# Gate and sum buffer in three parts, the copy out of PSUM ahead of the gate's mask, token loads in thirds, and second products dealt out by a plan

## The chip, the cores and the metric

One core of one Trainium2 chip runs the whole kernel. The metric is the device time of one execution in microseconds (us), as a median over runs. The engines are TensorE (PE, with its weight loads as PEld), VectorE (DVE), ScalarE (ACT), GpSimd (POOL) and SyncE (SP), which issues nearly all of the transfers.

## What is computed

```python
scores = scale * np.matmul(q, k.transpose(0, 1, 3, 2))        # 8 x 12 heads, 448 x 448, head_dim 64
scores = np.einsum('bhij,hg->bgij', scores, w_pre)            # heads are mixed before the softmax
attn = softmax(scores)                                         # max, exp, divided by the sum
attn = np.einsum('bhij,hg->bgij', attn, w_post)               # and mixed again after it
x = np.matmul(attn, v)  # -> 3584 tokens x 768
h = x @ w_in            # 768 -> 2048
g = h - np.tanh(h)      # the gate
out = g @ w_out         # 2048 -> 768
```

All is in float32. The kernel carries operands of matrix products as a high and a low part of a narrower type, and a product as three matmuls: high by high, high by low, low by high.

## The kernel before

The attention part fills the first 880 us or so of the span and is not touched; only its last places share the engines with the first block of the second part. The second part, the two large products with the gate between them, is where the change lies.

**Blocks.** The 3584 tokens are seven blocks of 512. Block 0 is computed plainly: 16 columns `f` of 128 hidden features, one after the other (`Block0.step`, L358). The six other blocks are taken in three pairs `s`, and a pair's two blocks and the halves of the weights go through a scheme with seven products in place of eight for a 2 x 2 split of the operands (Strassen-Winograd). Its operands, seven arrays called b11, b21, t2, t1, t3, b22, t4, are sums and differences of halves of the two blocks, each in a high and a low part.

**First products.** `pair_step` (L666) does one of eight steps `p` of a pair: seven products of nine matmuls each (three chunks of 128 rows, three matmuls a chunk) into two PSUM banks X and Y, in the order b11 X, b21 Y, t2 X, t1 Y, t3 X, b22 Y, t4 X. Some add to what is already in the bank, so a copy of X or Y on ACT or DVE has to have read the bank before the next product of that bank may start. The copy at L698 reads X after the third product (t2), and the fifth product (t3) waits for it. The weights of a product are one tile `wa` of 384 KB, loaded six products ahead (L626).

**Gate.** The gate of four hidden columns at a time is computed for two halves g1 and g2. The last parts of g1 and the whole of g2 run in the next step (`Late`, v0 to v5, L630 on): ACT does squares (L331, L332), the hyperbolic tangent (L336), another square (L337) and a mask (L347); DVE combines them (L340, L341, L344, L350) and overwrites the small arguments under the mask (L353). The tiles between them exist once each, so each engine waits for the other. In particular the mask (a3, L347) overwrites what L344 reads, so ACT gets to it only after DVE's L344. Four sums are then added (L655, L659, L660). Gate values and sums of one step are seven arrays of 128 x 512 in one tile `g` (1792 KB), of which there is one buffer. It is stored in DRAM (gs) by one transfer (L663, end of the step), and the next step's first write to it (L350 in v0) waits until that transfer has landed. In block 0 the first two arrays of the same tile take the gate of two columns, stored in go (L388).

**Second products.** The results are made of 200 units: 32 plain ones for block 0 and 56 for each pair. A unit is twelve matmuls into the banks y (L504 to L506, or L534 to L536). Two units share one weight tile `w` (768 KB, three buffers, L402, L418 or L421); two of a pair's units, or four plain ones, share one tile `gl` of gate values (512 KB, three buffers, L403 or L428), which ACT and DVE first split in a high and a low part (L448, L449). Loads are issued two tiles ahead. Results leave PSUM through tiles `c` and are stored by transfers of 192 KB (L519). The units of a pair can only run when the gate values of that pair are in DRAM, so the units of block 0 and of pair s fill PE during the steps of the pair after it.

**The order of the work** is written out by hand: each engine takes its instructions in the order in which the program calls them. After each product of a step, `rest(i)` runs `between(i)` (jobs that make the operands of the pair: `xq_jobs`, L570 on, eleven stages on ACT L576 and DVE L572, L579) and then a number of units. Before, a step of pair 0 gets 3 units, one of pair 1 or 2 gets 5.25 on the mean, and between two pairs stand 14 units (HELD 8 of the pair before, AHEAD 6 of the new one), into which the late gate's parts and five stages of the operands are dealt; the other stages run in step 0 of the next pair. In the tail, after the last pair, 14 such units and then 50 more run.

**Transfers.** SP issues in order. The token arrays of the next pair (five of 768 KB, L567) are loaded in the last step of a pair, each over two ranges of tokens (one where both lie in the same sequence), all three chunks in one transfer. The eight semaphores of SP's transfers are used in turn, so each issue first waits for the transfer eight before it. A load from gs waits for the stores of the same array region, and an issue that waits holds everything behind it.

Of the kernel before, what the change touches and what calls it, by code (L numbers as in the profile page):

```python
# [179 lines left out]
def kernel_body(  # L180
# [69 lines left out]

    ff = SimpleNamespace(w={}, x={}, xs={}, wa={}, w2={}, gr={}, gp={})

# [31 lines left out]
    def work(tag, n=2):  # L284
        return ff.rw.tile([P, n, TB], F32, name=tag, tag=tag)
# [70 lines left out]
    class Block0:  # L356
# [4 lines left out]
        def step(self, between=None):  # L361
# [19 lines left out]
            if f % 2:  # L381
                if old:
                    old.d2()
                    old.a3()
                    g = work("g", 7)[:, :2]
                    old.d3(g)
                    old.d4(g)
                    self.store = lambda: nc.sync.dma_start(gos[:, f - 3 : f - 1], g)  # L388
                self.old = Gate(self.h) if f < NF else None
            elif old:  # L390
                old.a1()
                old.a2()
                old.d1()


    class Results:
# [121 lines left out]
        def store(self, b, t, h, c):  # L518
            nc.sync.dma_start(  # L519
                out[b * TB + t * TT : b * TB + (t + 1) * TT, h * N2 : (h + 1) * N2], c.rearrange("p c n -> p (c n)")  # L520
            )

# [107 lines left out]
    class Late:  # L630
# [15 lines left out]

        def v3(self):
            self.g2.d2()
            self.g2.a3()
            self.g2.d3(self.g[:, 2:4])  # L650

        def v4(self):
            g = self.g
            self.g2.d4(g[:, 2:4])
            nc.vector.tensor_add(g[:, 4:6], g[:, 0:2], g[:, 2].unsqueeze(1).to_broadcast([P, 2, TB]))  # L655

        def v5(self):
            g = self.g
            nc.vector.tensor_add(g[:, 6], g[:, 1], g[:, 4])  # L659
            nc.vector.tensor_add(g[:, 2], g[:, 3], g[:, 6])  # L660

        def store(self):
            nc.sync.dma_start(gss[self.s][:, :, self.q], self.g)  # L663
            ff.stored[self.s] = self.q + 1

    def pair_step(s, q, late, units, between):  # L666
# [8 lines left out]
        def rest(i):  # L675
            between(i)
            res.units(units[i])

        X, Y = hbank(), hbank()
# [14 lines left out]
        if late:  # L694
            late.v2()
            late.v3()
        h23 = work("h23")
        nc.scalar.mul(h23[:, 0], X, -1.0)  # L698
        rest(2)

# [23 lines left out]
        g1.a3()  # L724
        if late:
            late.store()
        rest(6)
# [561 lines left out]

    def load_all_xq(s, names):  # L1290
        ba, bb = 2 * s + 1, 2 * s + 2
        for x, b, h in (("b11l", ba, 0), ("b21l", ba, 1), ("t3l", bb, 0), ("b22l", bb, 1), ("t4l", ba, 1)):
            if x in names:
                load_xq(x, b, h)

    xq = xq_jobs()
    res = Results()
    ff.n_wa, ff.stored = 0, [0] * NS

    def between0(f):  # L1300
        if 3 <= f <= 7:
            load_all_xq(0, (("b11l", "t3l", "b21l", "b22l", "t4l")[f - 3],))
# [12 lines left out]

    HELD, AHEAD = 8, 6
    late, left = None, 4 * NQ
    for s in range(NS):
        per_step = (left - HELD) / NQ
        due = 0.0  # L1320
        for p in range(NQ):

            def between(i):
                for _ in range(1 + (i == 0)):
                    next(xq, None)
                if p == NQ - 1 and s + 1 < NS:
                    for x, at in (("b11l", 0), ("b21l", 1), ("t3l", 4), ("b22l", 5), ("t4l", 6)):
                        if i == at:
                            load_all_xq(s + 1, (x,))

            units = []
            for i in range(7):
                due += per_step / 7
                units.append(int(due + 1e-6))
                due -= units[-1]
            late = pair_step(s, p, late, units, between)
        left = 7 * NQ - AHEAD
        if s + 1 < NS:
            xq = xq_jobs()
        jobs = [  # L1340
            [late.v0], [late.v1, late.v2], [late.v3], [late.v4], [late.v5, partial(next, xq, None)],
            [partial(next, xq, None)] * 2 + [late.store], [partial(next, xq, None)] * 2,
        ]
        for fs in jobs:
            for f in fs:
                f()
            res.units(2)
        late = None
    for _ in res.at:
        pass  # L1350

# [30 lines left out]
```

## Time and profile before

| | us |
|---|---|
| median of 3 runs (1884.4 to 1892.67) | 1887.47 |
| the profiled execution | 1885.07 |
| its span | 1883.3 |
| PE busy in it | 1724.8 |
| DVE busy | 1214.6 |
| ACT busy | 1146.1 |

The profiled execution lies 2.4 us below the median; its span is 1.8 us shorter than its time. Times in rows are us from the span's start; durations at the end of a group are in ns where it says "mean ns". A wait is told with the instruction that sat idle first and what released it behind the arrow. PEclk is the granted clock of TensorE as a share of full speed.

### The profile page before, as it was taken

The numbers are of one execution on the slowest core, as the hardware profiler recorded it, in microseconds if no ns is written. First come the engines' busy times: TensorE is split into PE (matmuls) and PEld (weight loads), VectorE is DVE, ScalarE is ACT, GpSimd is POOL, SyncE is SP. The second block draws the span as 40 slices with busy tenths as digits, with TensorE's granted clock in tenths as the row PEclk, the third lists the DMA queues.
The fourth block names the chain that finished last, engine by engine and source line by source line (L and its number), as shares of the span: only waits on it lengthen the run. The fifth ranks groups of instructions, "written<-read, shape, count | busy, mean of one in ns | idle before, by whom it ended". The sixth has DMA issues, their size and how long they took to land.

```text
span 1883.3 us, 40937 instructions
## 1 busy us (share of the span) xinstructions
PE 1724.8 (92%) x16068; PEld 1419.0 (75%) x16068; DVE 1214.6 (64%) x2119; ACT 1146.1 (61%) x2016; POOL 403.4 (21%) x574
## 2 busy tenths in 40 slices
PE   8999999999998999999968988888987988988898
PEld 6777777767776777777747777777877877877898
DVE  5776776676775776653867676757676767676333
ACT  5787777777786777674845554555554455555232
POOL 1454544544553454531000000000000000000000
PEclk9999999999998998999979999889999999999999
DMA  8769796887878597665956778858779858777897
GB/s 182 218 214 266 239 262 218 239 258 212 253 236 261 194 263 235 201 212 176 330 203 210 252 245 303 312 191 327 268 261 366 312 199 321 274 261 261 305 325 271
DMA packets 337743, 477.42 MB, mean 253 GB/s; under 512 B 103824, under 2 KB 262288, under 8 KB 337552
## 3 DMA queue, kind: packets, MB, share of 16 engines
q1 hardware_dynamic: 337244, 474.38, 77.0%
q8 instruction: 128, 2.10, 0.5%
q14 instruction: 63, 0.52, 0.1%
q10 hardware_dynamic: 308, 0.43, 0.1%
HBM read 277.09 MB, written 120.59 MB: 211 GB/s over the span
## 4 chain that ended last, share of the span: by engine, by line
PE 57%; DMA 17%; DVE 10%; ACT 9%; issue 3%; SPq 2%; POOL 2%; ACTq 0%; DVEq 0%; POOLq 0%
PE ps_o L951 12%; DMA gs<-g 8%; PE ps_m L993 7%; PE ps_p L912 7%; PE ps_q L868 5%; PE ps_h L315 4%; PE ps_h L316 4%; PE ps_h L318 4%; PE y L534 3%; PE y L536 3%; PE y L535 3%; DMA t<-s 2%; DMA w<-wo 2%; DMA vr<-in_v_dram 1%; DVE gl L449 1%
## 5 line engine op out<-in xcount | busy, mean ns | idle before, releaser
L951 PEld LDWEIGHTS ps_o<-wr,e 60*112 60x112 f32 (+1 forms) x5760 | 310.5, 177 | 43.1 <-POOL wr L934 18.4
L951 PE MATMUL ps_o<-wr,e 60*112 60x60 f32 (+1 forms) x5760 | 319.0, 261 | 15.7 <-ACT at L961 7.0
L921 DVE TENSOR_REDUCE mx<-ps_p 128x1 f32<-128x448 f32 x360 | 207.8, 619 | 184.0 <-PE ps_p L912 183.5
L923 ACT ACTIVATE e<-ps_p,mx 128x448 f32<-128x448 f32 x360 | 225.4, 633 | 97.4 <-DVE mx L921 95.4
L534 PE MATMUL y<-w,gh 128*128 128x384 f32 x672 | 231.4, 344 | 29.1 <-DMA w<-wo 14.0
L536 PE MATMUL y<-w,gl 128*128 128x384 f32 x672 | 230.1, 342 | 2.0 <-DVE gl L449 2.0
L535 PE MATMUL y<-w,gh 128*128 128x384 f32 x672 | 228.9, 341 | 0.0
L449 DVE TENSOR_TENSOR gl<-gl,gh 128x1024 fp32r<-128x1024 f32 x92 | 112.5, 1224 | 178.7 <-ACT gh L448 175.0
L961 ACT COPY at<-ps_o 112x960 f32<-112x960 f32 x156 | 153.8, 986 | 84.1 <-PE ps_o L951 83.5
L912 PE MATMUL ps_p<-t,wpre 60*64 60x448 f32 (+1 forms) x1440 | 184.1, 579 | 12.9 <-DMA t<-s 12.8
L993 PEld LDWEIGHTS ps_m<-at,vr 112*64 112x64 f32 x3072 | 150.4, 139 | 31.2 <-ACT at L968 12.4
L993 PE MATMUL ps_m<-at,vr 112*64 112x120 f32 (+1 forms) x3072 | 164.8, 264 | 8.3 <-ACT at L968 4.8
L448 ACT CAST gh<-gl 128x1024 fp32r<-128x1024 f32 x92 | 95.7, 1041 | 114.4 <-DMA gl<-gs 67.9
L331 ACT ACTIVATE u<-h 128x1024 f32<-128x1024 f32 x56 | 59.5, 1062 | 163.5 <-DVE h L708 83.1
L534 PEld LDWEIGHTS y<-w,gh 128*128 128x128 f32 x672 | 129.7, 193 | 37.7 <-ACT gh L448 23.9
L934 POOL TENSOR_TENSOR wr<-wpost,zs 128x120 f32<-128x120 f32 x180 | 70.3, 391 | 328.4 <-DVE zs L933 234.1
L535 PEld LDWEIGHTS y<-w,gh 128*128 128x128 f32 x672 | 129.8, 193 | 3.6
L536 PEld LDWEIGHTS y<-w,gl 128*128 128x128 f32 x672 | 128.9, 192 | 4.5 <-DVE gl L449 4.5
L347 ACT ACTIVATE qb<-u,bias 128x1024 f32<-128x1024 f32 x56 | 64.5, 1152 | 104.6 <-DVE qa L344 104.6
L868 PE MATMUL ps_q<-kk,qh 64*120 64x448 f32 (+1 forms) x768 | 126.3, 406 | 1.2 <-DVE kk L820 0.5
L868 PEld LDWEIGHTS ps_q<-kk,qh 64*120 64x120 f32 (+1 forms) x768 | 61.1, 179 | 86.0 <-issue 55.4
L873 DVE COPY s<-ps_q 120x448 f32<-120x448 f32 (+1 forms) x192 | 112.9, 616 | 14.2 <-PE ps_q L868 12.6
(174 smaller groups left out, 3376.2 us busy)
## 6 DMA issues: line engine op xcount, KB each, us to landing
t<-s SPq DMA_DIRECT2D x342, 210.0 KB
gs<-g SPq DMA_DIRECT2D x24, 1792.0 KB
gl<-gs SPq DMA_DIRECT2D x84, 512.0 KB
w<-wo SPq DMA_DIRECT2D x52, 768.0 KB
wa<-ss SPq DMA_DIRECT2D x96, 384.0 KB
w<-ts SPq DMA_DIRECT2D x48, 768.0 KB
wa<-wi SPq DMA_DIRECT2D x72, 384.0 KB
cr<-in_moe_w_in_dram SPq DMA_DIRECT2D x48, 256.0 KB
```

Of the source, the lines that this page charges most:

```text
L449: nc.vector.tensor_sub(lo, raw(lo), raw(hi))
L534: nc.tensor.matmul(y, gh[:, tok], wh, start=first, stop=False, skip_group_check=True)
L535: nc.tensor.matmul(y, gh[:, tok], wl, start=False, stop=False, skip_group_check=True)
L536: nc.tensor.matmul(y, gl[:, tok], wh, start=False, stop=last, skip_group_check=True)
L868: nc.tensor.matmul(ps[:n, :S], qx[a, hp, :], kx[a, hp % 2], start=(x == 0), stop=(x == 2))
L873: eng(sts[i][:n, 2 * hp + j, :], ps[:n, :S])
L912: nc.tensor.matmul(pss[r][halves[j], :], wpre[k, :], ts[j][k, :], start=True, stop=True)
L921: nc.vector.tensor_reduce(out=mx, in_=ps, axis=AX.X, op=ALU.max, negate=True)
L923: nc.scalar.activation(e, ps, AF.Exp, bias=mx, scale=1.0, accum_out=zs[:, 0, r : r + 1])
L951: nc.tensor.matmul(ps[:CP, j, c * GP : (c + 1) * GP].rearrange("p (h i) -> p h i", i=GI)[:, :, r * GH : (r + 1) * GH], e[k, c * CP : (c + ...
L961: nc.scalar.copy(ats[i0][:, :, :, at : at + 2 * GI].rearrange("p c h (j i) -> p j (c h) i", j=2), ps[:CP, :, : NC * GP].rearrange("p j (x ...
L993: nc.tensor.matmul(pv[j * D : (j + 1) * D, r, :n], vt[:, j, c, :], ats[i][:, c, 2 * hp + j, :n], start=(c == 0), stop=(c == NC - 1),)
```

## The change

1. The tile `g` of seven arrays becomes three: `ga` (two arrays, the gate g1), `gb` (two, the gate g2) and `gs` (three sums). Memory stays the same. `ga` is stored when two ticks have passed after v0, `gb` and `gs` two ticks after v5. In block 0 the gate alternates between `ga` and `gb`.
2. A tick passes after every unit and once at the end of each `rest`; `after(n, f)` puts off a call by n ticks. The stores of results (L519) are put off by two ticks too.
3. In `pair_step` the copy of X that was behind v2 and v3 (L698) is called between them, so on ACT it stands ahead of the mask.
4. Each token load is cut into its three chunks: `load_xq` issues six transfers where there were two, and they are dealt out two or so at a time.
5. Block 0 runs two more stages of the operands (columns 13 and 15). Between two pairs all eleven stages stand, two at a time.
6. The plan of the units: between pairs stand HELD + AHEAD = 18 and 18 units in place of 14, and 14 after the last pair. Step 0 of the three pairs gets 4, 6 and 5 units (FIRST); the other seven share 12, 34 and 37. So a step of pair 0 has one or two units where it had three, one of pair 1 four or five.

```diff
-                    g = work("g", 7)[:, :2]
+                    g = work(("ga", "gb")[f // 2 % 2])
...
+    def after(n, f):
+        ff.later.append([n, f])
+
+    def tick():
+        for x in ff.later:
+            x[0] -= 1
+        while ff.later and ff.later[0][0] <= 0:
+            ff.later.pop(0)[1]()
...
         def units(self, n):
             for _ in range(n):
                 next(self.at, None)
+                tick()
...
         def store(self, b, t, h, c):
...
+            after(2 if self.n_gr < len(self.grs) else 0, lambda: nc.sync.dma_start(to, c.rearrange("p c n -> p (c n)")))
...
         x_tiles(name)
-        for to, i, at in runs(b):
-            nc.sync.dma_start(raw(ff.xs[name])[:, :, to], xs[i][:, h * HK : (h + 1) * HK, at])
+        for c in range(HK):
+            for to, i, at in runs(b):
+                nc.sync.dma_start(raw(ff.xs[name])[:, c, to], xs[i][:, h * HK + c, at])
+            yield
...
         def v0(self):
-            self.g = work("g", 7)
+            self.ga = work("ga")
             self.g2.a1()
-            self.g1.d3(self.g[:, 0:2])
-            self.g1.d4(self.g[:, 0:2])
+            self.g1.d3(self.ga)
+            self.g1.d4(self.ga)
+            after(2, lambda: nc.sync.dma_start(gss[self.s][:, 0:2, self.q], self.ga))
...
         def v5(self):
...
+            after(2, self.store)
...
         def store(self):
-            nc.sync.dma_start(gss[self.s][:, :, self.q], self.g)
+            nc.sync.dma_start(gss[self.s][:, 2:4, self.q], self.gb)
+            nc.sync.dma_start(gss[self.s][:, 4:7, self.q], self.gs)
...
         if late:
             late.v2()
-            late.v3()
         h23 = work("h23")
         nc.scalar.mul(h23[:, 0], X, -1.0)
+        if late:
+            late.v3()
         rest(2)
...
-        if late:
-            late.store()
         rest(6)
...
-        if 6 <= f < NF and f % 2 == 0:
+        if 6 <= f < NF and f % 2 == 0 or f in (13, 15):
             next(xq, None)
...
-    HELD, AHEAD = 8, 6
+    HELD, AHEAD, FIRST = (16, 14, 10), (2, 4, 4), (4, 6, 5)
...
-                for _ in range(1 + (i == 0)):
-                    next(xq, None)
+                next(xq, None)
                 if p == NQ - 1 and s + 1 < NS:
-                    for x, at in (("b11l", 0), ("b21l", 1), ("t3l", 4), ("b22l", 5), ("t4l", 6)):
-                        if i == at:
-                            load_all_xq(s + 1, (x,))
+                    for _ in range((2, 2, 2, 0, 1, 3, 2)[i]):
+                        next(xl, None)
...
         jobs = [
-            [late.v0], [late.v1, late.v2], [late.v3], [late.v4], [late.v5, partial(next, xq, None)],
-            [partial(next, xq, None)] * 2 + [late.store], [partial(next, xq, None)] * 2,
+            [late.v0], [late.v1, late.v2], [late.v3], [late.v4], [late.v5, job], [job, job], [job, job], [job, job],
+            [job, job], [job, job],
         ]
+        n = HELD[s] + AHEAD[s]
+        for i in range(0, n, 2):
+            res.units(1)
+            for f in jobs.pop(0) if jobs else ():
+                f()
+            for _ in range(2):
+                next(xl, None)
+            res.units(1)
```

The order of ACT in a middle step of pair 1, before, from the copy of the first product (L682) to the copy of the third (L698); h, u, qa, qb and t are tiles of the gate, ps_h is bank X or Y, gh the high part of a unit's gate values:

```order
L682 COPY h_16165<-ps_h 128x512
L331 ACTIVATE u<-h_16035 128x1024
L332 ACTIVATE qa<-u,bias 128x1024
L336 ACTIVATE t<-h_16035 128x1024
L337 ACTIVATE qb<-u,bias 128x1024
L448 CAST gh<-gl 128x1024
L347 ACTIVATE qb<-u,bias 128x1024
L698 ACTIVATE h_16237<-ps_h 128x512
```

The same place of the same engine in the changed program, where line numbers are some 15 higher (L712 is the copy that was L698):

```order
L697 COPY h_16183<-ps_h 128x512
L331 ACTIVATE u<-h_16027 128x1024
L332 ACTIVATE qa<-u,bias 128x1024
L336 ACTIVATE t<-h_16027 128x1024
L337 ACTIVATE qb<-u,bias 128x1024
L712 ACTIVATE h_16234<-ps_h 128x512
L347 ACTIVATE qb<-u,bias 128x1024
```

The mask, L347, has moved behind the copy out of PSUM. (That no cast of gh stands there now comes from the other plan of the units.)

SP's issues around the store of the gate values in two steps of pair 0, before; wa, w and gl are the loads told above, gs_90 is pair 0's array in DRAM, wi, ss, wo and go are where the loads come from:

```order
L663 DMA gs_90<-g 896x1x512
L626 DMA wa<-wi_69 128x768
L626 DMA wa<-wi_70 128x768 x2
L403 DMA gl<-go 128x1024
L402 DMA w_14657<-wo_75 128x1536
L626 DMA wa<-ss_82 128x768 x4
L663 DMA gs_90<-g 896x1x512
```

The same queue over one step in the changed program:

```order
L651 DMA gs_90<-ga 128x2x512
L637 DMA wa<-wi_71 128x768
L637 DMA wa<-ss_83 128x768
L411 DMA w_14800<-wo_74 128x1536
L637 DMA wa<-ss_83 128x768 x2
L676 DMA gs_90<-gb 128x2x512
L677 DMA gs_90<-gs 128x3x512
L637 DMA wa<-ss_83 128x768
L637 DMA wa<-wi_71 128x768
L637 DMA wa<-wi_72 128x768
L651 DMA gs_90<-ga 128x2x512
```

The one store has become three, and `ga` leaves four products' loads ahead of `gb` and `gs`. SP's queue holds 137 rows more in all (928 in place of 791).

More of the change, by code (lines that the diff above doesn't have):

```diff
@@ L248, in kernel_body @@
     n_steps = sum(16 if x[2] is sums_in else 15 for x in quads)
-    ff = SimpleNamespace(w={}, x={}, xs={}, wa={}, w2={}, gr={}, gp={})
+    ff = SimpleNamespace(w={}, x={}, xs={}, wa={}, w2={}, gr={}, gp={}, later=[])
     def pool(name, bufs, side, stack=ctx):
@@ L1288, in kernel_body, with xq_loads @@
     xq = iter(())
-    def load_all_xq(s, names):
+    def xq_loads(s):
         ba, bb = 2 * s + 1, 2 * s + 2
         for x, b, h in (("b11l", ba, 0), ("b21l", ba, 1), ("t3l", bb, 0), ("b22l", bb, 1), ("t4l", ba, 1)):
-            if x in names:
-                load_xq(x, b, h)
-    xq = xq_jobs()
+            yield from load_xq(x, b, h)
+    xq, xl = xq_jobs(), xq_loads(0)
     res = Results()
@@ L1300, in between0 @@
     def between0(f):
-        if 3 <= f <= 7:
-            load_all_xq(0, (("b11l", "t3l", "b21l", "b22l", "t4l")[f - 3],))
+        if f >= 3:
+            for _ in range(4 if f % 2 else 2):
+                next(xl, None)
         if f in (10, 12):
@@ L1313, in kernel_body @@
     res.more_w2(2)
-    HELD, AHEAD = 8, 6
+    HELD, AHEAD, FIRST = (16, 14, 10), (2, 4, 4), (4, 6, 5)
     late, left = None, 4 * NQ
     for s in range(NS):
-        per_step = (left - HELD) / NQ
-        due = 0.0
         for p in range(NQ):
             def between(i):
-                for _ in range(1 + (i == 0)):
-                    next(xq, None)
+                next(xq, None)
                 if p == NQ - 1 and s + 1 < NS:
-                    for x, at in (("b11l", 0), ("b21l", 1), ("t3l", 4), ("b22l", 5), ("t4l", 6)):
-                        if i == at:
-                            load_all_xq(s + 1, (x,))
[L1331 to L1337, printed above, removed]
+                    for _ in range((2, 2, 2, 0, 1, 3, 2)[i]):
+                        next(xl, None)
+            if p == NQ - 1 and s + 1 < NS:
+                xl = xq_loads(s + 1)
+            many = FIRST[s] if p == 0 else (left - HELD[s] - FIRST[s]) * p // (NQ - 1) - (left - HELD[s] - FIRST[s]) * (p - 1) // (NQ - 1)
+            late = pair_step(s, p, late, [many * (i + 1) // 7 - many * i // 7 for i in range(7)], between)
+        left = 7 * NQ - AHEAD[s]
         if s + 1 < NS:
             xq = xq_jobs()
+        job = partial(next, xq, None)
         jobs = [
-            [late.v0], [late.v1, late.v2], [late.v3], [late.v4], [late.v5, partial(next, xq, None)],
-            [partial(next, xq, None)] * 2 + [late.store], [partial(next, xq, None)] * 2,
-        ]
+            [late.v0], [late.v1, late.v2], [late.v3], [late.v4], [late.v5, job], [job, job], [job, job], [job, job],
+            [job, job], [job, job],
+        ]
+        n = HELD[s] + AHEAD[s]
[4 more added lines that the diff above has]
+            for _ in range(2):
+                next(xl, None)
+            res.units(1)
         for fs in jobs:
@@ L1346, in kernel_body @@
                 f()
-            res.units(2)
         late = None
     for _ in res.at:
-        pass
+        tick()
+    while ff.later:
+        tick()
     E = mybir.EngineType
```

19 lines of the change are left out of this document (9 added, 10 removed).

## The prediction

> **What bounds the kernel now.** I read the page first, then the busy time by stage, then what PE waited for, then single steps. The page says that PE is the engine to look at:
>
> ```profile
> PE 1724.8 (92%) x16068; PEld 1419.0 (75%) x16068; DVE 1214.6 (64%) x2119; ACT 1146.1 (61%) x2016; POOL 403.4 (21%) x574
> ```
>
> The change leaves all before 880 us as it is, so the stages of the pairs are what counts. Busy time by stage, each cut within 1 us of the first matmul of a step (columns: length, busy time and instructions of each engine, granted clock, share of the DMA engines, GB/s):
>
> ```profile
> core 0: us, PE busy (x) PEld busy (x) DVE busy (x) ACT busy (x) POOL busy (x), PEclk, DMA share, GB/s
> 951.00:1000.00 49.00, 32.08 (x97) 23.55 (x98) 26.24 (x22) 19.92 (x21) 0.00 (x0) 0.72 0.45 157
> 1000.00:1145.00 145.00, 130.97 (x597) 107.95 (x596) 103.55 (x100) 80.29 (x88) 0.00 (x0) 0.95 0.70 238
> 1145.00:1210.00 65.00, 54.77 (x270) 48.11 (x270) 42.83 (x37) 31.84 (x40) 0.00 (x0) 0.92 0.92 325
> 1210.00:1248.00 38.00, 30.04 (x124) 24.48 (x123) 19.34 (x15) 17.64 (x21) 0.00 (x0) 0.82 0.63 233
> 1248.00:1418.00 170.00, 158.22 (x753) 139.33 (x753) 119.36 (x116) 94.65 (x110) 0.00 (x0) 0.97 0.79 282
> 1418.00:1489.00 71.00, 60.16 (x305) 54.76 (x304) 51.20 (x49) 32.79 (x33) 0.00 (x0) 0.95 0.94 335
> 1489.00:1528.00 39.00, 29.91 (x122) 25.09 (x122) 19.34 (x15) 17.50 (x21) 0.00 (x0) 0.87 0.64 228
> 1528.00:1695.00 167.00, 156.52 (x753) 138.01 (x752) 118.69 (x116) 94.74 (x110) 0.00 (x0) 0.98 0.79 280
> 1695.00:1879.00 184.00, 166.71 (x904) 159.31 (x902) 79.25 (x81) 62.28 (x71) 0.00 (x0) 0.98 0.83 293
> sum 928.00, PE 819.37 PEld 720.59 DVE 579.78 ACT 451.65 POOL 0.00; mean PE 91.04 PEld 80.06 DVE 64.42 ACT 50.18 POOL 0.00
> ```
>
> PE idles 108.6 of 928 us, and where it idles its clock sinks. What the same work takes without either shows in a step that lost nothing (seven products and five units, from b11 to the next b11) and in one unit:
>
> ```profile
> 1248.18 0.39 PE L315 MATMUL ps_h<-b11h,wa 128*128 128x512 f32 x1
> ...
> 1273.20 0.39 PE L315 MATMUL ps_h<-b11h,wa 128*128 128x512 f32 x1
> ...
> 1486.76 0.33 PE L534 MATMUL y<-w,gh 128*128 128x384 f32 x1
> ...
> 1488.84 0.39 PE L315 MATMUL ps_h<-b11h,wa 128*128 128x512 f32 x1
> ```
>
> A unit is 2.08 us, a step's seven products 25.02 - 5 x 2.08 = 14.6. All 24 steps and 200 units make 24 x 14.6 + 200 x 2.08 = 767 us. The 928 us thus hold 161 us of loss: 109 idle, 52 from the slow clock. That is the most a change of this kind can win. What PE waited for in these stages (total, times, longest), and the largest wait of DVE:
>
> ```profile
> PE ps_h L315 <- ACT h L698: 37.2, 15, 5.1
> PE y L534 <- DMA w<-wo: 14.0, 6, 5.8
> PE y L534 <- ACT gh L448: 12.1, 3, 7.9
> PE ps_h L315 <- ACT b22h L576: 10.6, 3, 4.4
> ...
> PE ps_h L316 <- DVE t2l L579: 4.2, 1, 4.2
> ```
>
> ```profile
> DVE g L350 <- DMA gs<-g: 73.4, 21, 8.2
> ```
>
> The first line is the copy of X behind the mask; DVE stands still for the one buffer of `g`, and that wait is what makes the mask late.
>
> **The middle steps.** One step of pair 0, DVE and ACT:
>
> ```profile
> 1125.94 1.23 DVE L350 TENSOR_TENSOR g<-qa,u 128x1024 f32<-128x1024 f32 x1 [2.82 <-DMA gs<-g]
> ...
> 1137.20 0.69 DVE L708 TENSOR_TENSOR h<-h,ps_h 128x512 f32<-128x512 f32 x1 [0.16 <-PE ps_h L318]
> ...
> 1141.87 1.22 DVE L340 SCALAR_TENSOR_TENSOR qa<-qa,h 128x1024 f32<-128x1024 f32 x1
> ...
> 1144.14 1.22 DVE L344 SCALAR_TENSOR_TENSOR qa<-qb,qa 128x1024 f32<-128x1024 f32 x1
> ```
>
> ```profile
> 1130.36 1.14 ACT L337 ACTIVATE qb<-u,bias 128x1024 f32<-128x1024 f32 x1
> ...
> 1134.12 0.58 ACT L698 ACTIVATE h<-ps_h 128x512 f32<-128x512 f32 x1
> ...
> 1137.92 1.06 ACT L331 ACTIVATE u<-h 128x1024 f32<-128x1024 f32 x1 [2.73 <-DVE h L708]
> 1139.01 1.15 ACT L332 ACTIVATE qa<-u,bias 128x1024 f32<-128x1024 f32 x1
> ```
>
> ACT was through with its square at 1131.50 and copied X only at 1134.12: ahead of the mask the copy comes 2.6 us sooner, and without the 2.82 us for `g` another 2.8. Either alone about covers this step's wait. What is added: the mask now stands behind the copy, so it can't start before the third product has ended and the copy's 0.58 us are over, and DVE's L353 and all behind it wait for the mask. In this step the product was over (L698's row names no wait of its own), and where units stand between the first products I take up to 2 us of DVE time, covered by the air of those steps (below). The two extra stores cost SP an issue each. `ga` leaves in the first products of a step and is written again a step later. `gb` and `gs` leave behind the fifth product and are written again behind the next step's third: five products and one to four units, 12 us or more, against a wait of at most 8.2 now; I count nothing for it in the middle steps, and up to 1 us if the landing is later.
>
> What is late next is the gate's own cycle. From L350 at 1125.94 to L708's end at 1137.89 are 11.95 us, two squares on ACT up to 1140.16 are 2.3, L340 to L344's end 3.5: 17.7 us, and the next L350. PE needs 14.6 + 12/7 x 2.08 = 18.2 in the shortened steps of pair 0, which hold one or two units, and about 25 in pairs 1 and 2. So pair 0 stands at the edge: DVE and ACT, which had 3 units of cover in a step, have one or two. With the split of a `gl` now and then I take 1 us a step, between 0 and 2.5. Loss in 1000 to 1145: 20 now, 6 then. In 1248 to 1418 and 1528 to 1695: 18 and 15 now, 3 each then (0 to 8), since the cycle has some 5 us of air there.
>
> **The first step of pair 0** (951 to 1000, loss 28). DVE:
>
> ```profile
> 960.80 1.23 DVE L350 TENSOR_TENSOR g<-qa,u 128x1024 f32<-128x1024 f32 x1 [3.47 <-DMA go<-g]
> ...
> 970.19 1.76 DVE L572 TENSOR_TENSOR xr<-b22l,t3l 128x1536 f32<-128x1536 f32 x1
> 971.86 2.35 DVE L449 TENSOR_TENSOR gl<-gl,gh 128x1024 fp32r<-128x1024 f32 x2
> ```
>
> The 3.47 go, and two stages (3.5 us) move under block 0, where DVE is nearly full, so perhaps half of that is gained: both splits end near 969 instead of 974.2. But the first unit now stands ahead of product t2, so PE waits for its split there with t2 behind it. Then come five products and four units, 10.4 + 8.3, some 3 us slow: about 990, with one unit more. Loss 16 (10 to 24).
>
> **Between the pairs** (1145 to 1248 and 1418 to 1528, loss 28 and 29). The waits for b22h and their like come from stages left over into step 0; all eleven now lie before it. The wait for gh hung on `g` through L331. The loads stopped for a store to land:
>
> ```profile
> 1478.27 0.57 SPq L663 DMA_DIRECT2D gs<-g  x1
> 1489.85 0.33 SPq L428 DMA_DIRECT2D gl<-gs  x1
> ```
>
> SP stood 11.6 us between the two. The load there wants the newest of the pair's values; with 18 units between the pairs it comes several units behind their store, so I count this at nothing, and at the 14.0 us for `w` in PE's list, tail included, if the store should slip behind. Against it stands the traffic. From the last step's start to the next pair there are 20 and 23 units, 57 and 63 us of PE. By tile sizes (token loads 3.9 MB, `wa` 2.8, gate stores 3.7, results 1.6, `w` 0.79 per two units, `gl` 0.52 per two or four) that is 12.0 MB beside 7.9 + 2.9 and 9.0 + 6.0: 22.8 and 27 MB, 400 and 430 GB/s. What transfers reach, 1145 to 1210 in 40 slices:
>
> ```profile
> GB/s 412 384 330 395 396 378 379 357 382 394 269 370 363 336 271 337 410 411 400 394 429 418 420 403 381 122 2 0 62 310 395 396 354 239 211 379 403 415 229 45
> ```
>
> About 390 where the queue is full. At that rate they take 58 and 69 us, 1 and 6 more than PE, part of it covered by tiles loaded ahead. And DVE has two subtractions of 1.76 and a split of 1.18 per two units there, 4.7 us against 4.2 on PE, over four such pairs of units: 2 us. With the slow clock behind each wait I take 9 and 11 of loss (5 to 25 each).
>
> **The tail** (1695 to 1879, loss 24): the gh waits and the load behind the last store go, the last waits for `w` and the end's drain stay: 8 (5 to 15).
>
> The sum of what stays: 16 + 6 + 9 + 3 + 11 + 3 + 8 = 56 of 161, so 105 us gained. The profiled execution took 1885.07, 2.4 less than the median and inside the runs: **1780 us**.
>
> The slow clock's part is carried along in proportion, since short waits bring it too:
>
> ```profile
> 1495.52 0.66 PE L534 MATMUL y<-w,gh 128*128 128x384 f32 x1 [2.40 <-DMA w<-wo]
> 1495.98 0.52 PE L535 MATMUL y<-w,gh 128*128 128x384 f32 x1
> 1496.30 0.52 PE L536 MATMUL y<-w,gl 128*128 128x384 f32 x1
> ```
>
> After 2.40 us of idle time, matmuls start 0.32 us apart. The Trainium skill, "TensorE: Matmul & The Clock Gate", section "What's actually happening", has the clock halved after at least one idle window of about 3.4 us. By that alone some nine waits would count, 15 us of slow clock by an estimate instead of 52, and the forecast would be near 1804; the rows show shorter waits doing it, so they decide.
>
> **The rivals.** *Transfers take the place of the waits* (0.2). Stages between pairs run at their present mean of 325 to 335 GB/s: 22.7 and 27 MB take 68 and 81 us, 29 more than PE's, 7 of which are in the sum. Small loads may be slow; the nearest, twelve of 32 and 224 KB:
>
> ```profile
> DMA packets 1881, 2.44 MB, mean 244 GB/s; under 512 B 973, under 2 KB 1741, under 8 KB 1880
> ```
>
> At 244 instead of 390 the 7.9 MB of pairs 1 and 2 cost 12 us more; with 12 of slow clock, 1780 + 22 + 12 + 12 = 1826. For it speaks the DMA share of 0.92 and 0.94 there, against it the slices at 400. By the Trainium skill, "DMA: Bandwidth & Descriptors", section "Measured", transfers of 64 KB reach 138 GB/s and of 1 MB 341: an estimate of 34 us more, 1814. No run yet shows such cuts beside full queues.
>
> *The gate's cycle bounds pair 0* (0.12): 2.5 us in each of six steps, 9 more than summed, and the split in the first step no sooner, 8 more: 1797. For it: 17.7 beside 18.2.
>
> *SP becomes the bound, slower* (0.04). 137 rows more stand in its queue, each waiting for the transfer eight before it, with the loads of `wa` and `w` behind them in the last step of a pair. With eight in flight and a landing of 11.6 us (the rows of the store) one goes out every 1.45 us; if each added one held PE up by that: 1780 + 199 = 1979. It decides from 105/137 = 0.77 us each. Against it: smaller transfers leave less in flight and land sooner, an issue itself took 0.33 to 0.57 us, and `wa` is asked for six products ahead.
>
> *The change does less than it says* (0.03): DVE waits for the landing of `gb` as it did for `g`, the copy's wait comes back as a wait for L708, and PE's order of units only moves the idle time. Then none of the 105 us comes: 1885. Against it: the 12 us between the store and the next write.
>
> **The numbers.** The forecast's own case has 0.61. With all the ends above on one side it would give 1749 or 1844; independent of each other (the root of the squares) 1768 or 1807. Several of the low ones have one cause, a gate that is never late, so I set 1755. The range 1755 to 1828 takes in the cycle and the transfers. A measurement of this kernel can tell about 0.5%, 9 us, from no change. Faster 0.93, same 0.03, slower 0.04.
>
> **What would show it.** Right: the line of L698 (now L712) gone from PE's waits, DVE's wait for the store under 15 us, steps of pair 0 near 19 us and of pair 1 near 25 (24.4 to 26), idle time of PE behind 951 near 40 us, no gap of 10 us between a store and the next load on SP. Wrong: PE waiting for `w` or `wa` for more than 30 us between the pairs, the DMA share above 0.95 there with PE under 85%, or DVE's L708 as PE's first releaser.

## The result and the profile after

The kernel after takes 1791.19 us (median of four runs, 1788.61 to 1794.49), the kernel before 1885.93 beside it. The ratio is 0.950, 95% interval 0.946 to 0.955: faster, by 95 us, with 1780 forecast and 1828 as the upper end of the range. The profiled execution of after took 1794.49 us, its span 1792.8; before it was 1885.07 and 1883.3, so between these two it is 91 us. The text below compares these two executions.

Busy time by stage in after, cut at the first matmul of the same steps as in the table of before, with block 0 ahead (columns: length, busy time and instructions of each engine, granted clock, share of the DMA engines, GB/s):

```profile
879.00:953.20 74.20, 63.79 (x270) 50.94 (x268) 50.85 (x42) 48.86 (x53) 0.00 (x0) 0.98 0.82 279
953.20:990.20 37.00, 27.65 (x112) 22.22 (x113) 25.89 (x22) 20.00 (x20) 0.00 (x0) 0.82 0.57 204
990.20:1104.00 113.80, 108.96 (x500) 88.41 (x499) 99.96 (x97) 77.38 (x86) 0.00 (x0) 1.00 0.82 281
1104.00:1169.40 65.40, 59.02 (x305) 50.87 (x304) 46.89 (x40) 34.32 (x44) 0.00 (x0) 0.95 0.96 336
1169.40:1198.40 29.00, 27.43 (x137) 24.42 (x136) 17.23 (x15) 13.88 (x15) 0.00 (x0) 1.00 0.82 288
1198.40:1351.40 153.00, 150.31 (x728) 133.25 (x727) 115.83 (x114) 94.06 (x110) 0.00 (x0) 0.99 0.86 302
1351.40:1430.80 79.40, 69.15 (x342) 64.96 (x341) 58.93 (x55) 39.87 (x41) 0.00 (x0) 0.91 0.97 356
1430.80:1456.10 25.30, 25.19 (x124) 22.21 (x123) 14.08 (x12) 13.69 (x17) 0.00 (x0) 1.00 0.82 275
1456.10:1608.60 152.50, 152.50 (x752) 136.14 (x751) 119.59 (x116) 94.13 (x108) 0.00 (x0) 1.00 0.85 306
1608.60:1789.40 180.80, 169.37 (x929) 162.49 (x927) 79.29 (x81) 64.31 (x75) 0.00 (x0) 0.99 0.85 306
```

The clock column says it at once: 1.00 or 0.99 in the middle steps of all three pairs, where it was 0.95 to 0.98, and PE busy for all of 152.5 us in pair 2. From 953.2 to 1789.4 PE idles 46.6 of 836.2 us (108.6 of 928 before). With the prediction's 767 us for the work, 70 us of loss are left of 161; what is not idle time of it, 23 us, is the slow clock. What is left lies in four rows: the first step, the last steps of pairs 0 and 1 (where the DMA share is 0.96 and 0.97), and the tail.

What PE waited for from 951 to 1790 (total, times, longest), and DVE's largest wait:

```profile
PE y L543 <- DMA w<-ts: 7.2, 5, 4.4
PE y L543 <- DMA w<-wo: 6.9, 5, 3.6
PE y L514 <- ACT gh L457: 6.3, 1, 6.3
PE y L514 <- DMA w<-wo: 6.2, 1, 6.2
PE ps_h L315 <- DMA wa<-wi: 3.8, 1, 3.8
```

```profile
DVE gl L458 <- ACT gh L457: 186.8, 71, 8.6
```

The copy of X (L712 now), 37.2 us and first before, is not among them: 1.6 us are left of it in three waits. DVE's 73.4 us for the store of `g` are gone; its wait for the cast, shown here, was 175.0 us before and is no work of the change. Five single waits of 3.6 to 6.3 us are the largest that PE has now.

A middle step of pair 0 and one of pair 1, each from its first matmul to that of the next:

```profile
1066.99 0.40 PE L315 MATMUL ps_h<-b11h,wa 128*128 128x512 f32 x1
...
1085.47 0.40 PE L315 MATMUL ps_h<-b11h,wa 128*128 128x512 f32 x1
```

```profile
1275.94 0.39 PE L315 MATMUL ps_h<-b11h,wa 128*128 128x512 f32 x1
...
1300.96 0.39 PE L315 MATMUL ps_h<-b11h,wa 128*128 128x512 f32 x1
```

18.48 us with two units, against 14.6 + 4.16 = 18.8 in theory, and 25.02 with five, which is the step without loss. SP behind the stores of the pair's last gate:

```profile
1370.96 0.46 SPq L677 DMA_DIRECT2D gs<-gs  x1
1371.85 3.57 SPq L530 DMA_DIRECT2D out_dram<-c  x4
...
1376.02 1.98 SPq L577 DMA_DIRECT2D t3l<-xs  x4
...
1378.99 0.43 SPq L437 DMA_DIRECT2D gl<-gs  x1
```

The next load of `gl` still comes 8 us behind the store, but SP does not stand still: stores, weights and token loads go out in between.

### The profile page after: what moved, and what is told of

It reads as the page before. It is cut to its first block, busy times and chain, and to the rows that moved or that the text cites. A ratio compares the mean times of both kernels' runs of the same rounds, so it can differ in the third digit from the quotient of the medians.

```text
span 1792.8 us, 41167 instructions
## 1 busy us (share of the span) xinstructions
PE 1691.1 (94%) x16068; PEld 1401.2 (78%) x16068; DVE 1215.1 (68%) x2119; ACT 1147.2 (64%) x2016; POOL 405.1 (23%) x574
## 4 chain that ended last, share of the span: by engine, by line
PE 60%; DMA 11%; ACT 10%; DVE 10%; issue 5%; POOL 2%; SPq 2%; ACTq 0%; DVEq 0%; POOLq 0%
PE ps_o L965 13%; PE ps_m L1007 8%; PE ps_p L926 7%; PE ps_q L882 5%; PE ps_h L315 4%; PE ps_h L316 4%; PE ps_h L318 4%; PE y L543 3%; PE y L545 3%; PE y L544 3%; DMA t<-s 2%; DVE qa L344 2%; DMA gl<-gs 1%; DMA w<-wo 1%; ACT gh L457 1%
## 5 line engine op out<-in xcount | busy, mean ns | idle before, releaser
L1007 PE MATMUL ps_m<-at,vr 112*64 112x120 f32 (+1 forms) x3072 | 165.7, 265 | 11.1 <-ACT at L982 5.9
L948 POOL TENSOR_TENSOR wr<-wpost,zs 128x120 f32<-128x120 f32 x180 | 70.6, 392 | 326.5 <-DVE zs L947 227.8
L347 ACT ACTIVATE qb<-u,bias 128x1024 f32<-128x1024 f32 x56 | 64.6, 1153 | 66.3 <-DVE qa L344 66.3
```

The source lines that it names most:

```text
L1007: nc.tensor.matmul(pv[j * D : (j + 1) * D, r, :n], vt[:, j, c, :], ats[i][:, c, 2 * hp + j, :n], start=(c == 0), stop=(c == NC - 1),)
```

## The experiments

Twelve runs, in three groups of four; each group ran with its own runs of the kernel before (medians 1879.7, 1879.3, 1883.4, beside 1885.9 in the result), so medians of different groups can differ by some 6 us for that alone; the ratios allow for it. For the table each profiled execution is cut at the same matmuls, and a stage's loss is its length minus 14.6 us a step and 2.08 a unit, as in the prediction. "Block 0" is a length, from the first matmul of its second column to that of the first step. "Step 0" is the first step of pair 0; "0", "1", "2" are steps 1 to 6 of a pair; "0 to 1" and "1 to 2" are the last step of a pair with the first of the next.

```
kernel          median   ratio [95%]             block 0  step 0   0    0 to 1   1    1 to 2   2    tail   loss
before          1885.9   1                         68.3    27.8   20.0   28.0   17.5   29.2   14.6  23.7   161
copy_only       1846.3   0.982  [0.979, 0.986]     68.6    24.7    4.6   26.4    8.4   34.3    5.4  24.2   128
split_only      1809.0   0.963  [0.958, 0.968]     68.4    27.0    2.8   21.9    2.1   24.4    2.0  16.2    96
copy_split      1807.8   0.962  [0.960, 0.965]     68.8    26.7   -1.4   23.6    0.2   25.0    0.2  13.3    88
old_plan        1807.0   0.961  [0.958, 0.963]     75.2    15.4   -1.4   24.4    0.2   29.2    0.2   9.7    78
one_buffer      1813.0   0.964  [0.959, 0.969]     75.9    13.6   13.5   15.3    6.5   18.2    1.6  17.3    86
copy_back       1802.9   0.960  [0.955, 0.964]     74.4    14.0   10.8   12.3   10.5   15.7    4.6  12.7    81
after           1791.2   0.950  [0.946, 0.955]     74.8    14.1    5.6   11.1    5.2   17.3    0.4  16.4    70
after_again     1794.7   0.954  [0.950, 0.958]     76.2    13.5    5.6   11.3    3.5   17.8    0.4  14.4    67
whole_loads     1787.0   0.951  [0.947, 0.954]     71.9    14.0    5.6    8.4    4.9   18.3    0.4  12.6    64
block0_loads    1789.7   0.952  [0.949, 0.954]     70.9    13.0    5.6   12.7    5.0   18.7    0.4   9.9    65
first_late      1790.5   0.953  [0.949, 0.957]     77.0    15.1    5.5   12.1    5.1   17.9    0.3  14.2    70
held_more       1794.8   0.954  [0.950, 0.959]     75.6    13.5    5.6   10.4    3.6   21.9    0.4  12.5    68
all_three       1786.1   0.950  [0.946, 0.954]     70.6    15.9    5.5    8.4    3.7   17.9    0.3  11.4    63
```

The stages are the sharper measure: this second column begins anywhere from 873.7 to 893.4 us in these executions, with the same code ahead of it, so a total carries several microseconds of chance from the attention part.

### The two halves of the middle steps, alone

**copy_only**, the kernel before with the copy of X moved:

```diff
         if late:
             late.v2()
-            late.v3()
         h23 = work("h23")
         nc.scalar.mul(h23[:, 0], X, -1.0)
+        if late:
+            late.v3()
```

> The kernel before with one edit: the copy of X stands ahead of the mask. Theory (either edit alone covers the wait in the middle steps, as the prediction said): the loss of the steps 1 to 6 of all pairs falls from 20 + 18 + 15 to about 6 + 3 + 3, the rest stays, so 1886 - 41 = 1845 us (1830 to 1860); PE's wait for the copy is under 10 us in all, DVE still waits over 50 us for the store of g. Rival (the wait only moves, since DVE still stands still for g): PE waits as long for L708 or the next sums instead, 1870 us or more.

1846.3 us, and what it waited for (PE, then DVE):

```profile
PE y L534 <- ACT gh L448: 18.6, 4, 9.3
...
PE ps_h L315 <- ACT h L697: 10.5, 9, 2.8
```

```profile
DVE g L350 <- DMA gs<-g: 68.8, 19, 9.2
```

DVE stands still for `g` as long as before, and PE's wait for the copy falls from 37.2 to 10.5 us. Steps 1 to 6 lose 18 us instead of 52, the boundaries nothing less (gh waits 18.6 instead of 12.1). The time is the expected one, the wait for the copy just above the expected 10. The rival, that the wait only moves, falls.

**split_only**, the kernel before with three buffers, `gb` and `gs` taken in v3 and v4 and stored where the one store stood, block 0's gate in `ga` and `gb` by turns, copy still behind the mask (the main lines):

```diff
-            self.g = work("g", 7)
+            self.ga = work("ga")
...
         def v1(self):
+            nc.sync.dma_start(gss[self.s][:, 0:2, self.q], self.ga)
             self.g2.a2()
```

> The kernel before with one edit: the buffer of gates and sums is three buffers, that of g1 leaves in the second product, the others where the one store stood. Theory (either edit alone covers the middle steps): the same 41 us there, and beside it the waits for gh that hung on g (12) and part of the 3.5 us of the first step: about 1886 - 55 = 1831 us (1815 to 1850); DVE's wait for a store under 15 us, PE's wait for the copy under 12 us. Rival (the mask is late for other reasons too, so the copy behind it still comes late): PE's wait for the copy stays at 18 us or more and the time above 1855.

1809.0 us, better than the expected range. PE's waits:

```profile
PE y L534 <- DMA w<-wo: 11.0, 5, 3.7
PE ps_h L315 <- ACT b22h L576: 10.4, 3, 4.4
PE ps_h L315 <- ACT h L700: 6.9, 4, 1.8
```

The wait for the copy is 6.9 us, without any move of the copy, so the rival (18 us or more) falls; the waits for gh are gone, and the tail loses 16 instead of 24. What stays is what this edit does not touch: the first step (27) and the boundaries, with the stages of step 0 (b22h).

**copy_split**, both edits in the kernel before:

> The kernel before with the two edits together: copy of X ahead of the mask, and three buffers with the early store of g1. Theory (the split has taken nearly all of the middle steps alone; alone it left 2.4, 1.9 and 1.9 us there): the copy adds about 5, 1804 us (1798 to 1808), first step and boundaries stay at 25 + 21 + 23 of loss. Rival (the 11 us that the copy was worth in the kernel after are worth as much here): 1798 or less.

1807.8 us, within 4 us of the expected 1804. The middle steps now lose nothing; by the stages the copy adds 9 us to the split (96.3 to 87.4), by the medians 1. No run takes back alone the two ticks by which after puts off the stores of results; they lie in the difference between this kernel and old_plan below, which is 1 us by the medians. The 34 us of the copy and the 71 of the split do not add up: they take the same wait.

### Undoing one part of the kernel after

**copy_back**: the copy behind the mask again.

```diff
             late.v2()
+            late.v3()
         h23 = work("h23")
         nc.scalar.mul(h23[:, 0], X, -1.0)
-        if late:
-            late.v3()
```

> The kernel after with the copy of X back behind the mask, all else as after. Theory (either alone covers): at most 9 us more than after, 1791 to 1800. Rival (the copy ahead of the mask is what wins the middle steps): PE's wait for the copy comes back with 1 to 2 us in most of 21 steps, 1815 us or more.

1802.9 us, 12 more than after and between the two expectations. Beside the second measurement of after, below, it is 8 more, with intervals that overlap; the stages settle it, as steps 1 to 6 lose 26 us instead of 11 and 9.5 in the two executions of after. PE waits for the copy, in ten places:

```profile
PE ps_h L315 <- ACT h L713: 16.8, 10, 3.2
```

One of them, ACT, DVE and PE in pair 1:

```profile
1294.40 1.22 DVE L344 SCALAR_TENSOR_TENSOR qa<-qb,qa 128x1024 f32<-128x1024 f32 x1
...
1295.71 1.15 ACT L347 ACTIVATE qb<-u,bias 128x1024 f32<-128x1024 f32 x1 [4.76 <-DVE qa L344]
1296.77 0.58 ACT L713 ACTIVATE h<-ps_h 128x512 f32<-128x512 f32 x1
...
1297.40 0.50 PE L315 MATMUL ps_h<-t3h,wa 128*128 128x512 f32 x1 [1.72 <-ACT h L713]
```

No store is in this chain. ACT stands 4.76 us for L344, DVE's ordinary third step of the gate, and the copy with it. L340 starts 9.1 us behind the step's first matmul here, as a split of `gl` stands ahead of it, and 7.1 in the step before, which loses nothing. In split_only, with the old plan, one step in each pair loses in this way, here about every second one.

**one_buffer**: one `g` of seven (in block 0 too), one store behind the sums, the rest as after.

```diff
-            self.ga = work("ga")
+            self.g = work("g", 7)
+            self.ga, self.gb, self.gs = self.g[:, 0:2], self.g[:, 2:4], self.g[:, 4:7]
...
-            nc.sync.dma_start(gss[self.s][:, 2:4, self.q], self.gb)
-            nc.sync.dma_start(gss[self.s][:, 4:7, self.q], self.gs)
+            nc.sync.dma_start(gss[self.s][:, :, self.q], self.g)
```

> The kernel after with one buffer of g and one store behind all sums, all else as after. Theory: the middle steps of pairs 1 and 2 lose nothing (copy ahead of the mask, 5 us of air), pair 0 has no air (17.7 beside 18.2) and pays the wait for g, 2.3 us in each of seven steps, 16; the boundaries pay the waits for gh and the stop of the loads behind the store, 5 to 12 each: 1791 + 16 + 17 = 1824 us (1808 to 1840). Rival (the copy alone is enough, as either alone covers): under 1803.

1813.0 us, in the expected range, and the rival falls. DVE's wait, and PE's first:

```profile
DVE g L350 <- DMA gs<-g: 26.6, 13, 3.4
```

```profile
PE ps_h L315 <- DVE h L700: 9.7, 6, 2.0
```

The wait for the store reaches PE mostly through the first sum of the next step (L700); four waits for the copy, 5.1 us, are left. Pair 0 loses 13.5 instead of 5.6, half of the 16 more that were expected; the boundaries only 4 and 1 more, where 17 were.

**old_plan**: 8 units held, 6 ahead, the others evenly, five stages between the pairs and the others in step 0; block 0, thirds, split and copy as after. Beside the lines below, the store of `gb` and `gs` goes one tick behind v5 instead of two.

```diff
-    HELD, AHEAD, FIRST = (16, 14, 10), (2, 4, 4), (4, 6, 5)
+    HELD, AHEAD = (8, 8, 8), (6, 6, 6)
...
-                next(xq, None)
+                for _ in range(1 + (i == 0)):
+                    next(xq, None)
```

> The kernel after with the units dealt out as before (8 held, 6 ahead, evenly over the steps) and the operand stages again partly in step 0 of the next pair; block 0, thirds, split and copy as after. Theory: the boundaries lose 45 us again instead of 27, the steps of pair 0 lose 2 instead of 5, so 1791 + 15 = 1806 us. Rival (the plan only moves the idle time, and what split and copy leave is the traffic's): 1797 or less.

1807.0 us: the plan is worth 12 to 16. PE's waits have the stage of step 0 back:

```profile
PE y L543 <- DMA w<-wo: 13.3, 8, 5.8
PE ps_h L315 <- ACT b22h L587: 8.8, 2, 4.4
```

The boundaries lose 24 and 29 instead of 11 and 17, pair 0 seven less. Beside copy_split, which has the same plan but block 0 and the loads as before, the times are the same: what the stages moved into block 0 win in the first step (27 to 15) goes for more than half in block 0 itself, with its loads in thirds (69 to 75).

### The token loads, and what is left

**whole_loads**: each array whole, at the place of its first third. **block0_loads**: only the loads of block 0 as before, whole and in the old order.

```diff
-        for c in range(HK):
-            for to, i, at in runs(b):
-                nc.sync.dma_start(raw(ff.xs[name])[:, c, to], xs[i][:, h * HK + c, at])
-            yield
+        for to, i, at in runs(b):
+            nc.sync.dma_start(raw(ff.xs[name])[:, :, to], xs[i][:, h * HK : (h + 1) * HK, at])
+        for c in range(HK):
+            yield
```

> The kernel after with each token array loaded whole at the place of its first third, places and order of all else as after. Theory: between the pairs the thirds win little, since the queue is full either way: within 5 us of after there; in block 0 the third of t3 that its first stage waits for comes sooner, 2 to 4 us: 1786 to 1791. Rival (whole arrays of 768 KB hold up w and wa between the pairs): 5 to 8 us at each boundary, 1800 or more.

> The kernel after with the five token loads of block 0 as before (whole, b11, t3, b21, b22, t4, one a column from column 3), all else as after. Theory (block 0's 6.4 us come from t3 that arrives too late for its first stage, which stalls DVE and ACT, and PE behind them): block 0 takes 69 us instead of 74.7, 1786 us. Rival (they come from the two more stages there and from the transfers that the earlier gate stores and loads meet): block 0 stays above 73 us, 1791.

1787.0 and 1789.7 us, 1 to 4 below after, which the medians can't tell from it; whole_loads is as expected, its rival falls. The stages can, in one place: block 0 takes 71.9 and 70.9 us, and 74.4 to 77.0 in all seven executions with thirds in it. In after the first stage is held up:

```profile
906.79 1.76 DVE L583 TENSOR_TENSOR xr<-t3l,b11l 128x1536 f32<-128x1536 f32 x1 [2.75 <-DMA t3l<-xs]
```

Two things changed for t3: it is asked for behind b21 and no longer ahead of it, and in thirds, the last of which goes out one column ahead of its use. whole_loads, with the new order, waits 0.90 us there; block0_loads, with the old one, has no such wait. The expectation for block0_loads, 69 us, and its rival, above 73, both miss its 70.9. That DVE's wait is what reaches PE isn't shown: what PE itself waits for in block 0 is mostly weights (2.97, 1.90 and 3.81 us in after, 1.83, 0.87 and 4.05 in block0_loads).

Between the pairs the size of the loads changes little. The last step of pair 1 in whole_loads, beside 79.40 us, 0.97 and 356 GB/s with thirds:

```profile
1360.60:1441.30 80.70, 69.70 (x342) 65.81 (x341) 60.21 (x56) 39.63 (x41) 0.00 (x0) 0.89 0.97 354
```

The last step of pair 0 is 2 to 3 us shorter in the two kernels with whole loads than in after, whose row has 65.40 us, 0.96 and 336 GB/s. In all_three (below):

```profile
1101.90:1164.60 62.70, 58.52 (x306) 50.48 (x305) 46.89 (x40) 34.34 (x44) 0.00 (x0) 0.97 0.98 351
```

**after_again**, the kernel after unchanged, **first_late** (the first two lines), **held_more** (the last two; the stages behind the second gate take one slot more) and **all_three** (both, and whole loads as in whole_loads):

```diff
+            if s == p == 0:
+                units = [0, 0, 0, 1, 1, 1, 1]
...
-    HELD, AHEAD, FIRST = (16, 14, 10), (2, 4, 4), (4, 6, 5)
+    HELD, AHEAD, FIRST = (16, 18, 10), (2, 4, 4), (4, 6, 5)
```

> The kernel after once more, unchanged, as the measure for the others of this call and for what one execution's stages are worth. Theory (the tail's loss of 15 and block 0's 74.7 us are in part one execution's chance): 1787 to 1794 us, tail loss anywhere from 8 to 16. Rival (they are the kernel's own): tail loss 14 to 16 and block 0 74 to 75 us again.

1794.7 us (1786.5 to 1801.2), tail 14.4, block 0 76.2. Block 0's length is the kernel's own, so the theory falls there. The tail, nearly the same code in all kernels made from after, loses 9.7 to 17.3 in their executions, so half of it can be chance.

> The kernel after with the four units of the first step of pair 0 behind its products t1, t3, b22 and t4 instead of b21, t1, b22 and t4. Theory (the 14 us lost there are the first unit that waits for gh and gl with four products queued behind it): PE fills the wait with t2 and t1, the step loses 6 to 9 instead of 14, 1791 - 6 = 1785 us. Rival (the products behind wait for the same engines: the copies and stages stand behind the last gate of block 0): the step loses 12 or more, no change.

1790.5 us; the step loses 15.1 instead of 14.1, so the rival was right. ACT and PE in it:

```profile
970.59 1.15 ACT L347 ACTIVATE qb<-u,bias 128x1024 f32<-128x1024 f32 x1 [1.58 <-DVE qa L344]
971.64 0.56 ACT L697 COPY h<-ps_h 128x512 f32<-128x512 f32 x1
...
972.26 0.52 PE L315 MATMUL ps_h<-t2h,wa 128*128 128x512 f32 x1 [3.74 <-ACT h L697]
...
982.00 0.50 PE L514 MATMUL y<-w,gh 128*128 128x512 f32 x1 [3.62 <-ACT gh L457]
```

The one wait of 6.3 us has become one for the copy of the first product, which stands on ACT behind block 0's last gate, and one for gh, which stands behind the casts of the stages. ACT, not the place of the unit, holds that step.

> The kernel after with 18 instead of 14 units of pair 1 held back for the boundary to pair 2, and the last two operand stages one at a time. Theory (boundary 2 loses 17 us because DVE and ACT have two stages per two units, 4.7 us against 4.2, and the transfers are 6 us more than PE's work): with four units more the boundary loses 8 to 11, the middle steps of pair 1 stay without loss (4.3 units, 23.6 us beside a gate's cycle of 17.7): 1784 us. Rival (the loss there is the clock and single late loads of w): no change, 1789 or more.

1794.8 us, no change; the boundary loses 21.9 instead of 17.3. Its last step of pair 1, 27 units:

```profile
1344.10:1436.90 92.80, 78.17 (x390) 73.43 (x389) 66.46 (x59) 44.50 (x45) 0.00 (x0) 0.93 0.93 333
```

PE's first releaser in that stretch of held_more:

```profile
PE y L543 <- DMA w<-ts: 7.5, 2, 4.0
```

Four units more, 8.3 us of work, make the step 13.4 us longer. Units bring their own `w` and `gl`, 2.6 MB here, so they do not relieve a stretch whose transfers are full; but at 356 GB/s that is 7.5 us, and the rate fell to 333, so bytes alone do not give the 13.4. The theory that two stages per two units are what is late there finds no support (only the last two were spread).

> The kernel after with the two edits above and whole token arrays. Theory: 6 from the first step, 6 from boundary 2, 4 from block 0: about 1776 us (1770 to 1785). Rival: the edits find no path of their own and it stays at 1787 or more.

1786.1 us (1781.2 to 1795.4), just outside the expected range and below its rival's 1787. It has the lowest median and, from the start of block 0 on, the shortest trace (900.3 us, against 911.0 and 908.9 in the two of after), but whole_loads alone makes 902.4 and block0_loads, whole only in block 0, 902.7, and in each of these three the tail is 4 to 7 us shorter than in the first execution of after, which may be chance; the interval of its ratio overlaps those of after and after_again, so it is not shown to beat after.

## Why the prediction was right, and where not

**Right: the mechanism and its place.** Forecast were 20 + 18 + 15 of loss in the middle steps falling to 6 + 3 + 3; measured 5.6, 5.2 and 0.4. In pair 0 PE waits for DVE's sums and the copy, 4.9 us, in keeping with the forecast; in pair 1, 4.6 of the 5.2 us lie in the one step with a wait of 2.19 us that has no known releaser (below), so there the size came by luck. The first step was set at 16 and lost 14.1; that it ends at 990.2, with about 990 forecast, is chance, as it began 1.5 us later. "Either alone about covers this step's wait" holds for the split in the steps of before, where it leaves 7 us of 52, and for the copy in part, which leaves 18. It does not hold in the steps of after, where undoing the copy costs 12 us and undoing the split 22; the prediction had seen only that pair 0 has no air. It did not weigh the two edits against each other: of the 95 us the split makes some 70 alone, the copy nothing that the medians show beside it under the old plan, and 12 under the new one.

**Mis-sized: the boundary from pair 1 to 2**, 11 forecast, 17.3 measured (9 and 11.1 at the other). The step that failed is "about 390 where the queue is full". The bytes were right (27 and 22.8 MB forecast; 356 GB/s over 79.4 us are 28.3, 336 over 65.4 are 22.0), the rate was nearer the best slices of 1.6 us (the first 25 of the row, all before its gap, have a mean of 377), and a whole stretch makes 336 and 356 with the DMA engines at 0.96 and 0.97. At these rates the forecast bytes take 68 and 76 us, for 56 and 62 of PE's work and 65 and 79 measured, the first rival in a smaller form. How late loads become waits of PE shows in that step:

```profile
1384.10 1.04 ACT L457 CAST gh<-gl 128x1024 fp32r<-128x1024 f32 x1 [4.55 <-DMA gl<-gs]
1385.17 1.23 DVE L458 TENSOR_TENSOR gl<-gl,gh 128x1024 fp32r<-128x1024 f32 x1 [6.88 <-ACT gh L457]
1386.01 0.66 PE L543 MATMUL y<-w,gh 128*128 128x384 f32 x1 [4.45 <-DMA w<-ts]
...
1398.06 1.15 ACT L347 ACTIVATE qb<-u,bias 128x1024 f32<-128x1024 f32 x1 [2.49 <-DVE qa L344]
1399.79 0.41 PE L543 MATMUL y<-w,gh 128*128 128x384 f32 x1 [2.95 <-ACT qb L347]
```

`gl` lands late, DVE stands 6.88 us for its split with the last gate queued behind, the mask is late by that and by two more such waits (1.93 and 1.24 us), and PE's next wait ends behind the mask. That full transfers set the length there is argued. For it: in ten of the table's fourteen executions this step moved 24.3 to 28.6 MB in 67.5 to 80.7 us, always at 351 to 361 GB/s and a share of 0.97 or more, so there its length follows its bytes. The other four do not fit as well: held_more and all_three, with 31 MB, made 333 and 350 GB/s, before and copy_only 336 and 330, at shares of 0.93 to 0.96. A kernel with the token loads outside that step was not tried.

**Mis-sized: the tail**, 8 forecast, 16.4 measured, 14.4 once more. Its waits are single tiles of `w`, the largest 3.58 us, and its drain; since other kernels with the same tail lost 9.7 to 17.3, the forecast lay below all of them, and one execution says little on it.

**Missed: block 0**, counted at nothing. It takes 74.8 us instead of 68.3. With whole loads 70.6 to 71.9, so about 4 us are the thirds; the other 2 to 3 go with the two more stages there, which no run separated. The prediction followed the two moved stages into block 0 and did not ask what the loads, cut and in another order, do to the first stage there, which had not moved.

The sum: stages 70.1 against 56 is 14.1 late, block 0 6.5 late, the attention part 5.0 early and the span's last part 1.0 shorter by chance: 14.6 of the 14.5 us between 1780 and the profiled execution. Without the attention part's chance it would be some 5 us more.

**Forecast signs.** L712 gone from PE's list but for 1.6 us, the store gone from DVE's, steps of 18.5 and 25.0 us, idle time of 46.6 us for 40, no gap of 10 us between a store and the next load on SP: all came. Of the signs of being wrong, half of one came: the DMA share passed 0.95 between the pairs (0.96 and 0.97), with PE busy for 90% and 87% and not under 85. PE waited 6.4 and 4.4 us for `w` in the last steps of pairs 0 and 1, far from 30.

**The clock.** It came in proportion as forecast: 52 us slow beside 109 idle before, 23 beside 47 after. A single wait in pair 1:

```profile
1247.24 0.41 PE L543 MATMUL y<-w,gh 128*128 128x384 f32 x1 [2.19 <-issue]
...
1247.69 0.52 PE L545 MATMUL y<-w,gl 128*128 128x384 f32 x1
1248.01 0.52 PE L543 MATMUL y<-w,gh 128*128 128x384 f32 x1
```

Behind 2.19 us of idle time the matmuls again start 0.32 us apart (0.17 in a unit without loss, 2.08 us by twelve), as behind the prediction's 2.40. By the Trainium skill, "TensorE: Matmul & The Clock Gate", section "What's actually happening", a wait this short would not count; five waits in PE's list above pass its 3.4 us, and at 15 us for nine waits, as the prediction had it, they would make 8 of the 23, an estimate. The rows speak against it again.

**The rivals.** "Transfers take the place of the waits" is the one that had a part of it right, at 8 us instead of 46. By the Trainium skill, "DMA: Bandwidth & Descriptors", section "Measured", cut loads would have cost 34 by the prediction's estimate. The runs do not bear it out: whole_loads is 4 us faster by the median (8 beside after_again), of which block 0 makes 3 to 4, and its two boundaries lose 3 us less and 1 more. The gate's cycle cost pair 0 at most the 5.6 us that it lost. SP's added issues cost nothing that shows: whole_loads takes the cut token loads away and the boundaries stay within 3 us. They are also fewer than the prediction counts: in the traces SP issues 1260 transfers instead of 1152, 108 more (60 of token loads, 48 of stores); the 137 rows more are of a list in which like issues in a row stand as one. At its 1.45 us each that rival would have cost 157 us and not 199. "The change does less" falls with the first table.

## What to carry to other kernels

When two edits take the same wait, measure each alone and each undone: here they gave 34 and 71 us alone, 12 and 22 undone, and none of the four numbers says what the others are. Take the rate of a stretch that is full of transfers from a whole stretch of that kind and not from its best slices, and follow a load that is cut or moved to the operation that waits for it, also where that operation has not moved. Compare stages cut at the same instruction when totals carry chance from a part that nobody changed.

## What the runs showed of the hardware

With token loads of 32 to 224 KB or whole ones the last step of pair 1 moved the same 354 to 356 GB/s at a DMA share of 0.97. There the size of these few loads among tiles of 384 to 768 KB did not set the rate. In the last step of pair 0 it may have a small part: whole_loads and all_three moved 348 and 351 GB/s, the kernels with the same stores and cut loads 328 to 339.

The 2.19 us at 1245 us, for which the profile names no releaser ("issue"), come back with 2.16 to 2.20 us at the same matmul in after_again, whole_loads, block0_loads and first_late; in old_plan and held_more, whose units lie elsewhere, there is no such wait. PE's order alone does not bring it: copy_back and one_buffer have the same order, and PE idles 0.33 and 0.54 us there, behind longer waits for the copy earlier in that step (1.72 and 3.28 us instead of 0.34). What it is stays open.
